# A rewritten issue order in a fused scan-attention and two-layer feed-forward kernel

## The chip, the cores and the metric

One core of one Trainium2 chip. The metric is the device time of one execution in microseconds (us), median of several runs.

## What is computed

A chunked linear attention with decay feeds two feed-forward layers. The reference, cut (4 batches, 8 heads, 768 positions, head size 32, state size 16):

```python
# attention, per chunk: Cc, Bc, xc, la = log(clip(a)), cum = cumsum(la)
M = einsum('bhin,bhjn->bhij', Cc, Bc) * exp(cum_i - cum_j) * causal
y = einsum('bhij,bhjd->bhid', M, xc) + (Cc @ state) * exp(cum)
state = exp(sum(la)) * state + sum_j Bc_j xc_j * exp(cum_last - cum_j)
# on 3072 tokens of 256 features
h = max(x @ w1, x @ w2, x @ w3)              # 768 wide
x = h @ w_out
out = (sigmoid(x @ w_gate) * (x @ w_val)) @ w_out2   # 1536 wide
```

## The kernel before, in words

The attention works on 8 chunks (c) of 96 positions. A chunk has 32 batch-heads, in 8 groups of four, so a step k = 8c + g is one group of one chunk, 64 steps in all. The feed-forward part works on 6 token tiles (t) of 512 tokens. A tile of the first layer has 6 slices (m) of 128 hidden features. Token tile 0 needs chunk 0 and the first half of chunk 1.

The attention, the preparation of the first layer's weights, token tiles 0 to 3 and the first slice of tile 4 are issued in an order written out by hand, the string `ORDER` (L52). `in_order` (L710) reads it word by word; `emit` (L655) maps a word to instructions. Each word is issued behind the last instructions of all words before it, so every engine, and SP's queue of transfers, runs its own instructions strictly in the written order, each one when its inputs and its buffer are there. The rest of token tile 4, tile 5 and the second layer follow from loops (L746, L866), which the change does not touch. The words, by engine:

- SP (SyncE), transfers: `a` loads the decays compactly, `astore` (L683) stores them clipped as the DRAM table `ad`. `LdN` (`load_decay`, L284) loads decay tile N, spread over 128 partitions; tiles 0 and 1 come from the input, the later ones from `ad`. There are four buffers of this kind, so LdN waits for the last uses of tile N-4. `LBc`, `LCc` load B and C of chunks 0 and 1, `pk` a small constant, `Lxch` (L294) x (first part) and a B layout (second part) of chunk c, half h. `Lbc` loads B and C of a later chunk, `Pdcp` (L666) distributes its bfloat16 parts. `Lwamh` (L593) loads half a weight tile of slice m in two parts.
- ACT (ScalarE): `kK` masks C for step K (L341); `Pcp` makes a bfloat16 part (L671); `sga`, `rawa`, `ra`, `hia` (L601 to L615) decode a weight tile; `H` rounds y to the high half of a split operand (L398); `E` takes a token product out of its bank (L642); `h` rounds the hidden tile (L646).
- DVE (VectorE): `clipN` clips decay tile N (L652); `DNa`, `DNb` are its two scans (L303), one for a step each; `mK` multiplies the scores of step K by the decays (L375); `T` transposes the state into the next chunk's x tile, rows of which it overwrites (L428); `X` makes the low half of y (L402); `stta` decodes weights (L609); `U`, `V` take the maximum with the other two products (L644).
- POOL (GpSimd): `bxK` state factors of step K (L364), `Q` the rest after a bfloat16 part (L673), `adda` (L612) and `loa` (L618) of weight tiles, `l` the low half of the hidden tile (L648). Those listed in `ON_DVE` run on DVE.
- PE (TensorE): `SK` the scores of step K: for k < 16 in float32 (L352), from step 16 on four bfloat16 products (L355). `yK` the outputs and state of a step (L385), from step 24 on of four steps together. `G` and `F` are the four and two terms of one token product, `N` and `O` those of the down product, all with split float32 operands (L461). `I` is an idle product on zeros and ones whose result nobody reads (L706).

Scores and token products share one pool of three PSUM banks (L348, L632), taken in turn. A bank comes free when `m`, `E`, `U` or `V` has read it. The state factors and weighed scores of a step use one of eight `mt` buffers.

Of the kernel before, what the change touches and what calls it, by code (L numbers as in the profile page):

```python
# [52 lines left out]
LB0 K Lwa00#0 a clip LC0 pk delta Lwa00 sga00 rawa00 stta00 Ld0 clip0 k6 Ld1 k2 k4 D0b S2 ra00 k5
clip1 D1a m2 adda00 I0 astore hia00 Lb2 P20 k0 D0a k1 I1 I2 Lx00#0 Lx00 bx2 Q20 k3 D1b Ld2 D2b I3
I4 I5 I6 LC1 S0 m0 S3 k7 bx3 m3 bx0 S1 m1 P21 Ld3 S5 m5 k9 I7 k8 D2a bx1 Lwa01#0 Lwa01 k13 k11 S7
loa00 D3a D3b m7 Lx01#0 sga01 rawa01 S4 m4 S6 m6 y3 Q21 Lwa10#0 Lx01 bx4 stta01 ra01 y4 Ld4 D4a y0
# [1 line left out]
Lx10#0 Lx10 y7 bx6 y6 H01 Lwa11#0 Lwa11 D5b bx11 D5a S11 S10 m11 S9 ra10 S8 T00 bx10 m10 y11 y10
adda10 Ld6 hia01 m9 bx9 y9 m8 hia10 bx8 y8 H10 Ld7 sga11 rawa11 X01 ra11 Lwa20#0 Lwa20 sga20 X10
loa10 loa01 Lwa21#0 Lwa21 D7a rawa20 D6b S13 m13 G000 F000 G001 F001 stta11 adda11 E00 sga21  # L60
rawa21 U00 ra20 Lwa30#0 Lwa30 stta20 stta21 Lx11#0 Lx11 G002 F002 G010 F010 hia11 loa11 ra21 k12
Lwa31#0 sga30 Lwa31 V00 G011 F011 G012 F012 E01 D7b bx14 h00 adda20 bx15 S12 rawa30 U01 V01 Ld8
l00 hia20 Ld9 ra30 sga31 Lx20#0 Lx20 adda21 stta30 D6a hia21 m12 Lwa41#0 loa20 rawa31 ra31 N00 O00
stta31 loa21 Lwa40#0 Lwa40 adda30 hia30 G020 F020 loa30 adda31 G021 F021 P22 k15 G022 F022 T10 h01
D8a E02 U02 bx16 V02 Lwa41 sga41 Lwa50#0 Lwa50 sga40 S14 m14 rawa40 ra40 stta40 l01 hia31 adda40
hia40 Pd21#0 S15 rawa41 loa31 G030 F030 h02 bx12 E03 Pd22#0 Pd22 N01 O01 T01 bx13 D9a bx18 G031
F031 Pd21#1 m15 y15 y13 Pd21#2 ra41 D8b bx17 sga50 l02 stta41 adda41 rawa50 ra50 stta50 loa40 U03
hia41 y12 G032 F032 N02 O02 Pd20#0 Pd20#1 Pd20#2 Pd20#3 D9b V03 Pd20#4 G040 F040 loa41 Pd20 E04
Pd21 S19 m19 S17 m17 y14 Ld10 Lwa51#0 h03 S16 G041 F041 m16 adda50 hia50 loa50 Lwa51 sga51 rawa51
D10a l03 Lx21#0 Lx21 Ld11 Lx31#0 U04 S20 m20 ra51 G042 F042 V04 h04 S18 m18 G050 F050 E05 N03 O03  # L70
S22 Lb3 stta51 S23 adda51 hia51 bx19 y18 y16 D11a Ld12 D10b bx21 m22 loa51 y17 D11b m23 y19 H11
X11 G051 F051 S21 P30 G052 F052 l04 T11 bx23 y23 Lx31 m21 bx22 H20 X20 y21 U05 bx20 y20 y22 H21
Lx30#0 X21 Q30 V05 h05 Lx30 Pd30#0 D12a bx24 Lx41#0 Lx41 N04 O04 D12b bx25 Pd30#1 Pd30#2 G100 F100
T20 G101 F101 P31 Q31 E10 U10 G102 F102 V10 P32 l05 G110 F110 E11 N05 O05 f0 Pd30#3 Ld13 Ld14 D13b
D14a D13a G111 F111 h10 G112 F112 G120 F120 l10 N10 O10 U11 V11 G121 F121 h11 l11 Pd30#4 Pd30 bx27
E12 Pd32#0 Pd31#0 Pd31#1 Pd31#2 Pd31 Pd32 S27 m27 Lb4 U12 P40 G122 F122 V12 S24 D14b Pd40#0 bx29
m24 Q40 G130 F130 N11 O11 h12 l12 G131 F131 S25 m25 E13 G132 F132 U13 V13 S26 h13 l13 P41 Pd40#1
Pd40#2 Pd40#3 m26 N12 O12 Ld15 D15a D15b bx26 G140 F140 E14 S28 m28 G141 F141 Ld16 bx31 bx28 T21
Lx40#0 Q41 Pd40#4 bx30 P42 S29 G142 F142 U14 Lx40 m29 V14 S30 m30 G150 F150 E15 Ld17 D17a S31
Pd42#0 Pd42 G151 F151 Ld18 Pd40 y27 H30 m31 bx34 y31 H31 X31 D18b X30 D16a U15 G152 F152 Pd41#0  # L80
h14 l14 N13 O13 V15 h15 Ld19 D19b D16b D19a D18a G200 F200 E20 N14 O14 G201 F201 U20 G202 F202
# [6 lines left out]
h24 Ld22 Ld23 Pd60#0 Pd60#1 l23 Pd60#2 S40 m40 G250 F250 E25 S43 G251 F251 bx41 D22a m43 T40
Pd60#3 y39 H41 X41 Pd61#0 bx43 y43 H50 X50 G252 F252 Pd61#1 N23 O23 D22b Ld24 l24 Q61 U25 V25
Pd61#2 G300 F300 S45 m45 G301 F301 N24 O24 Ld25 D24a Lx60#0 bx45 P62 h25 l25 Pd62#0 Pd62 Pd60#4  # L90
D23a E30 U30 G302 F302 V30 S44 m44 N25 O25 G310 F310 D25b D23b S47 bx46 m47 D24b h30 Pd60 G311
F311 E31 U31 S46 m46 Lb7 bx44 Pd61 l30 G312 F312 Ld26 V31 P70 f2 bx47 S51 m51 G320 F320 h31 Pd70#0
Pd70#1 Q70 Pd70#2 Pd70#3 Pd70#4 Lx60 S49 P71 G321 F321 T41 D25a Ld27 y47 E32 m49 U32 Q71 P72 bx50
G322 F322 S48 m48 Pd71#0 N30 O30 Lx61#0 V32 S50 D26b H51 m50 Lx61 G330 F330 E33 S52 D26a m52 G331
F331 X51 bx49 S53 G332 F332 bx48 m53 U33 V33 Ld28 T50 h32 D27a bx51 Ld29 S54 G340 F340 Lx70#0 m54
l31 E34 N31 O31 G341 F341 D29b bx53 Pd72#0 Pd72 S55 D27b m55 T51 h33 G342 F342 U34 V34 bx52 Pd71#1
bx54 Ld30 D30a l33 bx55 y51 y55 H61 X61 Lx70 bx59 Pd71#2 G350 F350 Pd71 l32 Pd70 S61 G351 F351
D30b m61 H60 X60 Ld31 D31b E35 U35 S63 Lx71#0 Lx71 T61 bx60 G352 F352 N32 O32 m63 G400 F400 E40
h34 D29a bx58 V35 N33 O33 D28a bx56 S56 m56 S58 l34 G401 F401 D28b m58 bx57 S57 U40 N34 O34 m57
# [874 lines left out]
```

## Time and profile before

| | before |
|---|---|
| median of 3 runs | 546.4 us (545.87 to 546.89) |
| the profiled execution | 546.38 us |
| its span, first to last instruction | 544.6 us |
| PE busy | 523.3 us (96%) |
| DVE busy | 401.1 us (74%) |
| ACT busy | 313.8 us (58%) |
| POOL busy | 90.4 us (17%) |

The profiled execution's own time is 1.8 us more than its span, which runs from its first instruction to its last. Busy time is the union of an engine's instructions. A matmul's end is modelled, so a busy PE is not PE at its peak. "Idle before" gives how long an engine stood still ahead of an instruction, and after an arrow what ended the wait.

### The profile page before, as it was taken

What the parts mean: (1) busy time and instruction counts of PE and PEld (TensorE: products, weight loads), DVE (VectorE), ACT (ScalarE), POOL (GpSimd) and SP (SyncE); (2) the same over time, 40 slices, a digit from 0 to 9 for tenths busy, and PEclk for the clock granted to TensorE, in tenths of its full rate; (3) what the DMA queues carried; (4) which work ended last, traced back from release to release, by engine and by line L of the source; (5) the groups of instructions that cost most, each with busy time, mean ns of one, the idle gap of its engine ahead of it and who ended that gap; (6) DMA issues with size and microseconds to landing.
All of it is one profiled execution on the core that took longest, in us unless ns stands there. A gap on an engine that the chain in (4) does not pass through costs nothing.

```text
span 544.6 us, 7902 instructions
## 1 busy us (share of the span) xinstructions
PE 523.3 (96%) x2897; PEld 418.2 (77%) x2898; DVE 401.1 (74%) x682; ACT 313.8 (58%) x551; POOL 90.4 (17%) x127
## 2 busy tenths in 40 slices
...
GB/s 209 289 308 214 211 158 164 162 151 138 204 182 139 222 17 201 186 46 148 78 40 0 2 0 1 1 40 39 2 0 1 0 1 78 1 0 0 2 0 78
DMA packets 33895, 50.53 MB, mean 93 GB/s; under 512 B 3392, under 2 KB 19904, under 8 KB 33856
## 3 DMA queue, kind: packets, MB, share of 16 engines
...
q8 instruction: 23, 0.38, 0.3%
...
## 4 chain that ended last, share of the span: by engine, by line
PE 82%; DVE 7%; DMA 5%; ACT 3%; issue 2%; SPq 0%; POOL 0%; DVEq 0%; POOLq 0%; ACTq 0%
PE u L461 22%; PE o L851 17%; PE ug L820 15%; PE uv L820 15%; PE o L461 7%; PE y L385 2%; PE s L352 2%; DVE dec L303 2%; PE s L355 1%; DMA bc<-in_bch 1%; DMA bx<-in_bn 1%; DMA dec<-ad 1%; DVE t_a L609 1%; DVE mt L375 1%; DVE s L644 1%
## 5 line engine op out<-in xcount | busy, mean ns | idle before, releaser
L461 PE MATMUL u<-xt_hi,w_a 128*128 128x512 f32 x432 | 121.6, 402 | 1.7 <-DVE w_a L618 0.5
L820 PE MATMUL ug<-xt_hi,w_g 128*128 128x512 f32 x252 | 92.0, 390 | 0.3 <-ACT ug L823 0.2
L461 PEld LDWEIGHTS u<-xt_hi,w_a 128*128 128x128 f32 x432 | 77.3, 188 | 19.0 <-DVE w_a L618 1.4
L820 PE MATMUL uv<-xt_hi,w_v 128*128 128x512 f32 x252 | 91.1, 390 | 0.0
L851 PE MATMUL o<-hi,w_d 128*128 128x512 f32 x288 | 78.4, 389 | 0.0
L461 PE MATMUL u<-xt_lo,w_a 128*128 128x512 f32 x216 | 66.9, 391 | 0.4 <-DVE xt_lo L402 0.4
L303 DVE TENSOR_TENSOR_SCAN dec<-dec,delta 128x388 f32<-128x388 f32 x64 | 59.5, 949 | 4.5 <-DMA dec<-ad 4.3
L851 PEld LDWEIGHTS o<-hi,w_d 128*128 128x128 f32 x288 | 54.1, 188 | 11.3
L895 DVE TENSOR_TENSOR lo<-y,hi 128x512 fp32r<-128x512 f32 x72 | 49.2, 687 | 16.1 <-ACT hi L894 15.2
L820 PEld LDWEIGHTS ug<-xt_hi,w_g 128*128 128x128 f32 x252 | 47.3, 188 | 11.2 <-ACT ug L823 0.7
L820 PEld LDWEIGHTS uv<-xt_hi,w_v 128*128 128x128 f32 x252 | 47.3, 188 | 10.7 <-DVE y L828 0.4
L894 ACT CAST hi<-y 128x512 fp32r<-128x512 f32 x72 | 44.5, 620 | 13.2 <-DVE y L891 12.0
L820 PE MATMUL ug<-xt_lo,w_g 128*128 128x512 f32 x126 | 49.1, 389 | 0.0
L820 PE MATMUL uv<-xt_lo,w_v 128*128 128x512 f32 x126 | 49.0, 389 | 0.0
L891 DVE TENSOR_TENSOR y<-uv,y 128x512 f32<-128x512 f32 x36 | 24.8, 688 | 32.9 <-PE uv L820 32.5
L461 PEld LDWEIGHTS u<-xt_lo,w_a 128*128 128x128 f32 x216 | 40.5, 188 | 9.7 <-DVE xt_lo L402 0.9
L851 PE MATMUL o<-lo,w_d 128*128 128x512 f32 x144 | 45.6, 391 | 0.0
L825 ACT COPY sv<-uv 128x512 f32<-128x512 f32 x36 | 21.2, 588 | 34.9 <-PE uv L820 34.7
L375 DVE TENSOR_TENSOR mt<-s,dec 128x384 f32<-128x384 f32 x64 | 34.6, 549 | 8.8 <-PE s L355 7.2
L644 DVE TENSOR_TENSOR s<-u,s 128x512 f32<-128x512 f32 x50 | 34.1, 682 | 8.4 <-PE u L461 7.3
L828 DVE TENSOR_TENSOR y<-ug,y 128x512 f32<-128x512 f32 x36 | 24.8, 689 | 21.0 <-ACT y L825 15.0
L461 PE MATMUL o<-hi,w_a 128*128 128x512 f32 x144 | 39.6, 397 | 0.0
...
## 6 DMA issues: line engine op xcount, KB each, us to landing
...
```

What stands on the lines that cost most here:

```text
L303: dve.tensor_tensor_scan(out=f, data0=f, data1=delta.rearrange("p u w -> p (u w)"), initial=0.0, op0=ALU.mult, op1=ALU.add)
L352: pe.matmul(ps[:, q, 0:CH], bcf[c][:, 128 * q:128 * q + 128], cm[:, k % MASKED, q], start=True, stop=True)
L375: last[0] = dve.tensor_tensor(out=m[:, :, 0:CH], in0=ps[:, :, 0:CH], in1=dc[:, :, 1:LW], op=ALU.mult)
L461: pe.matmul(ps, w[int(e == 1)], a_lo if e == 2 else a_hi, start=start, stop=stop)
L644: evict[1] = dve.tensor_tensor(out=s, in0=banks_of[t, m, 1 + (kind == "V")], in1=s, op=ALU.max)
L820: turn[0] = pe.matmul(ps, w, x, start=new and e == 0, stop=e == 2, skip_group_check=not new)
L825: evict[0] = act.copy(self.temp(1 if i == 6 else 2), ps)
L828: evict[1] = dve.tensor_tensor(out=self.t[k], in0=ps, in1=self.t[k], op=ALU.add)
L851: turn[0] = pe.matmul(acc2[t][d], w, x, start=n == 1 and e == 0, stop=n == M2 and e == 2)
L891: evict[1] = dve.tensor_tensor(out=g, in0=v, in1=g, op=ALU.mult)
L894: act.copy(hl[0], g)
L895: dve.tensor_tensor(out=hl[1], in0=g, in1=hl[0].bitcast(F32), op=ALU.subtract)
```

## The change

`ORDER` is replaced by another order of the same words; seven idle products (I6 to I12) are left out, so there are 974 words instead of 981. `ON_DVE` gets another list: 17 words instead of 15. Nothing else changes: the same transfers, scans, scores and products, with other neighbours. Where bfloat16 scores follow a token or down product, a place begins: there are 44 such places in the old order and 18 in the new one. At the start, `a`, x of chunk 0 (first half), `astore`, B, C, `pk` and decay tiles 0 and 1 now stand ahead of the first weight load. The diff, cut to the head, two stretches in the middle and at the end, and the lists:

```diff
-LB0 K Lwa00#0 a clip LC0 pk delta Lwa00 sga00 rawa00 stta00 Ld0 clip0 k6 Ld1 k2 k4 D0b S2 ra00 k5
-clip1 D1a m2 adda00 I0 astore hia00 Lb2 P20 k0 D0a k1 I1 I2 Lx00#0 Lx00 bx2 Q20 k3 D1b Ld2 D2b I3
-I4 I5 I6 LC1 S0 m0 S3 k7 bx3 m3 bx0 S1 m1 P21 Ld3 S5 m5 k9 I7 k8 D2a bx1 Lwa01#0 Lwa01 k13 k11 S7
-loa00 D3a D3b m7 Lx01#0 sga01 rawa01 S4 m4 S6 m6 y3 Q21 Lwa10#0 Lx01 bx4 stta01 ra01 y4 Ld4 D4a y0
-y2 y1 H00 X00 D4b I8 I9 Lwa10 bx7 sga10 rawa10 stta10 k14 I10 I11 LB1 I12 k10 adda01 Ld5 bx5 y5
...
-bx36 S37 m37 D17b Lx51#0 G220 F220 E22 h21 l21 S35 m35 Lx50#0 G221 F221 U22 P52 S38 m38 N20 O20
-G222 F222 S36 D20b D20a V22 h22 m36 G230 F230 E23 bx35 y35 H40 G231 F231 U23 Pd51 S39 G232 F232
...
-h35 l35 S62 D31a m62 G402 F402 S60 m60 N35 O35 bx61 T60 S59 bx63 m59 V40 bx62 y63 H71 X71 y59 H70
-X70
+a clip K Lx00#0 Lx00 astore LB0 delta LC0 pk k0 Ld0 clip0 D0a S0 m0 k6 Ld1 bx0 k2 clip1 D1a D1b
+bx3 Lwa00#0 S2 D0b k1 k4 m2 Lwa00 k3 sga00 rawa00 S1 I0 bx1 stta00 ra00 LC1 k10 adda00 k5 I1 I2 I3
+m1 k8 I4 Ld2 D2b hia00 S4 k12 D2a m4 Lb2 Ld3 D3b y1 k7 loa00 Lwa01#0 P20 Lwa01 S3 m3 S5 m5 k13 LB1
+sga01 rawa01 S7 S6 bx2 y2 Q20 P21 Q21 S8 Ld4 Ld5 Lx01#0 Lx01 k11 ra01 bx4 D3a bx6 m7 y3 y0 stta01
+m6 bx5 k9 D4b P22 Lx10#0 Lx10 S10 bx7 D4a adda01 S11 Lwa10#0 D5a m10 m8 H00 T00 X00 k15 D5b Lwa10
...
+h15 D18a Lb5 N14 D18b Pd40 P50 Q50 Lx41#0 Lx41 T31 bx36 E20 l15 G201 G202 F201 D16a bx32 O14 F202
...
+S38 m38 S36 m36 bx34 Lb6 S37 m37 Pd51#2 Pd51 Ld20 D20a D20b Pd52#0 Pd52 y35 S39 m39 h22 P60 H40
+G231 F231 G232 O21 Ld21 D21b D21a F232 U23 V23 Lx51#0 bx38 Pd60#0 Ld22 D22b Ld23 N22 Lx51 l22 Q60
...
+Pd70#0 Pd70#1 f2 G320 S50 m50 F320 E32 N30 G321 F321 Ld27 D27b Q71 bx51 bx49 Lx61#0 G322 F322 Lx61
+G330 P72 F330 E33 U32 V32 S49 m49 S54 y47 Pd71#0 Pd71#1 D27a m54 bx53 y51 Pd71#2 Pd72#0 S53 H60
+m53 H51 h31 S55 l31 D26a bx52 S52 m55 m52 O30 h32 Ld28 D28b G331 F331 N31 Ld29 D28a bx56 G332
+Lx71#0 T51 G340 F332 U33 Ld30 V33 D30b l32 O31 N32 h33 l33 F340 T60 E34 G341 F341 U34 G342 G350
+G351 Pd70#2 Pd70#3 X60 bx54 Lx71 bx55 D29a X51 Ld31 D31b F342 O32 N33 Pd70#4 V34 h34 F350 D31a
...
-ON_DVE = """Q20 loa10 adda20 adda21 loa21 adda40 l02 loa40 l05 l10 l11 l12 l21 l25 l35""".split()
+ON_DVE = """adda10 adda11 adda21 l00 loa30 adda40 l02 loa40 adda50 loa50 Q31 l12 Q41 l20 l24 l30 l33""".split()
```

## Rows read from the trace of the kernel before

**Rows 1.** The page: busy us of each engine (share of the span), instructions.
```profile
PE 523.3 (96%) x2897; PEld 418.2 (77%) x2898; DVE 401.1 (74%) x682; ACT 313.8 (58%) x551; POOL 90.4 (17%) x127
```

**Rows 2.** Table by stretch: length, busy us (instructions), clock, DMA share, GB/s.
```profile
core 0: us, PE busy (x) PEld busy (x) DVE busy (x) ACT busy (x) POOL busy (x), PEclk, DMA share, GB/s
...
11.00:79.30 68.30, 63.00 (x497) 47.94 (x498) 65.07 (x103) 45.88 (x78) 40.23 (x48) 1.00 0.82 234
79.30:209.00 129.70, 127.48 (x944) 96.85 (x942) 102.72 (x178) 44.25 (x72) 45.69 (x62) 1.00 0.70 149
209.00:545.00 336.00, 331.28 (x1456) 271.83 (x1452) 232.22 (x400) 217.55 (x390) 0.27 (x1) 1.00 0.11 38
```

**Rows 3.** Timeline of DVE: start us, duration us, instruction, [idle before <-releaser].
```profile
5.44 0.35 DVE L652 TENSOR_SCALAR a<-a 64x384 f32<-64x384 f32 x1 [5.44 <-DMA a<-in_ah]
8.46 0.69 DVE L609 SCALAR_TENSOR_TENSOR t_a<-raw_a,sg 128x512 int32<-128x512 int32 x1 [2.67 <-ACT raw_a L603]
11.08 1.19 DVE L652 TENSOR_SCALAR dec<-dec 128x768 f32<-128x768 f32 x1 [1.93 <-DMA dec<-in_ah]
```

**Rows 4.** Timeline of PE: the first products of token tiles 0 and 1.
```profile
35.12 1.18 PE L461 MATMUL u<-xt_hi,w_a 128*128 128x512 f32 x4
...
79.33 1.09 PE L461 MATMUL u<-xt_hi,w_a 128*128 128x512 f32 x4
```

**Rows 5.** Timeline of SP's queue: first issue, the decay tiles, and the store.
```profile
0.74 0.38 SPq L576 DMA_DIRECT2D y<-in_bch  x1
...
3.84 0.94 SPq L287 DMA_DIRECT2D dec<-in_ah  x2
5.82 0.48 SPq L683 DMA_DIRECT2D ad<-a  x1
```

**Rows 6.** From issue to landing: B loads (L576), compact decays (L680), decay tiles (L287).
```profile
DMA to landing us min/median/max: 2.7/3.7/4.7
...
DMA to landing us min/median/max: 3.8/3.8/3.8
...
DMA to landing us min/median/max: 3.3/5.6/7.8
```

**Rows 7.** Groups of DVE instructions: busy us, mean ns | idle before.
```profile
L303 DVE TENSOR_TENSOR_SCAN dec<-dec,delta 128x388 f32<-128x388 f32 x64 | 59.5, 949 | 4.5 <-DMA dec<-ad 4.3
...
L648 DVE TENSOR_TENSOR lo<-s,hi 128x512 fp32r<-128x512 f32 x8 | 5.4, 678 | 1.6 <-ACT hi L646 1.6
...
L612 DVE CUSTOM_DVE_ANT_0 r_a<-t_a,r_a 128x1024 uint16<-128x1024 uint16 x3 | 2.5, 830 | 0.1
...
L673 DVE TENSOR_TENSOR bc<-bc,parts 128x896 f32<-128x896 f32 x1 | 1.1, 1066 | 0.0
```

**Rows 8.** Chain of waits, token products, scores (s), outputs (y): start us, us, what.
```profile
65.96 0.28 PE s L355 x4
...
96.47 1.36 PE o L461 x6
...
99.18 0.19 PE s L355 x4
99.37 1.47 PE u L461 x6
...
198.55 0.36 PE s L355 x8
...
205.68 0.90 PE y L385 x32
206.59 1.58 PE u L461 x6
```

**Rows 9.** Waits: who waited for whom, us in total, times, the longest.
```profile
PEld L355 <- issue: 13.3, 45, 1.1
```

More of the change, by code (lines that the diff above doesn't have):

```diff
@@ L52 @@
 ORDER = """
[L53 to L56, printed above, removed]
-y2 y1 H00 X00 D4b I8 I9 Lwa10 bx7 sga10 rawa10 stta10 k14 I10 I11 LB1 I12 k10 adda01 Ld5 bx5 y5
@@ L58 @@
[L58 to L81, printed above, removed]
@@ L82 @@
-bx33 Pd41#1 Pd41#2 bx32 Pd41 S33 m33 l15 N15 O15 Lb5 P50 Q50 P51 Pd51#0 bx37 Pd50#0 V20 G210 F210
-E21 h20 l20 Q51 Pd51#1 T31 S32 m32 T30 Pd50#1 G211 F211 Ld20 S34 m34 f1 U21 G212 F212 V21 Pd51#2
-bx36 S37 m37 D17b Lx51#0 G220 F220 E22 h21 l21 S35 m35 Lx50#0 G221 F221 U22 P52 S38 m38 N20 O20
-G222 F222 S36 D20b D20a V22 h22 m36 G230 F230 E23 bx35 y35 H40 G231 F231 U23 Pd51 S39 G232 F232
-Pd52#0 Pd50#2 Ld21 Pd50#3 m39 Pd50#4 Pd50 Lx50 bx38 l22 X40 bx40 bx39 V23 N21 O21 h23 Pd52 G240
-F240 E24 S42 D21a m42 D21b N22 O22 Lb6 P60 Q60 G241 F241 U24 Lx51 S41 bx42 m41 P61 G242 F242 V24
@@ L88 @@
[L88 to L99, printed above, removed]
@@ L100 @@
-h35 l35 S62 D31a m62 G402 F402 S60 m60 N35 O35 bx61 T60 S59 bx63 m59 V40 bx62 y63 H71 X71 y59 H70
-X70
+a clip K Lx00#0 Lx00 astore LB0 delta LC0 pk k0 Ld0 clip0 D0a S0 m0 k6 Ld1 bx0 k2 clip1 D1a D1b
+bx3 Lwa00#0 S2 D0b k1 k4 m2 Lwa00 k3 sga00 rawa00 S1 I0 bx1 stta00 ra00 LC1 k10 adda00 k5 I1 I2 I3
+m1 k8 I4 Ld2 D2b hia00 S4 k12 D2a m4 Lb2 Ld3 D3b y1 k7 loa00 Lwa01#0 P20 Lwa01 S3 m3 S5 m5 k13 LB1
+sga01 rawa01 S7 S6 bx2 y2 Q20 P21 Q21 S8 Ld4 Ld5 Lx01#0 Lx01 k11 ra01 bx4 D3a bx6 m7 y3 y0 stta01
@@ new lines @@
+m6 bx5 k9 D4b P22 Lx10#0 Lx10 S10 bx7 D4a adda01 S11 Lwa10#0 D5a m10 m8 H00 T00 X00 k15 D5b Lwa10
+y4 y5 y7 y6 H01 m11 S9 sga10 S13 bx8 y8 bx10 rawa10 ra10 y10 Lwa11#0 m9 bx9 y9 Lwa11 bx11 hia01
+stta10 adda10 loa01 y11 H10 X10 I5 sga11 hia10 Ld6 D6b Lwa20#0 m13 rawa11 Lwa20 sga20 rawa20 G000
+G001 G002 Ld7 loa10 Ld8 ra11 X01 F000 F001 E00 F002 stta11 stta20 G010 F010 ra20 adda20 adda11
+hia11 loa11 hia20 loa20 U00 E01 V00 Lwa21#0 Lwa21 Lx11#0 D7b sga21 rawa21 G011 F011 U01 G012 F012
+h00 Lx11 bx13 D6a D8b Lwa30#0 ra21 Lwa30 sga30 stta21 V01 rawa30 stta30 ra30 Pd20#0 G020 F020 E02
@@ new lines @@
+adda21 Ld9 l00 bx15 G021 F021 U02 S12 m12 k14 hia21 bx12 S15 m15 Lwa31#0 Lwa31 adda30 loa21 S14
+hia30 loa30 sga31 rawa31 stta31 D7a m14 D9a G022 F022 V02 Lwa41#0 ra31 adda31 N00 h01 l01 Lwa40#0
+Lwa41 Lwa40 sga41 rawa41 O00 hia31 Lwa50#0 Lwa50 sga40 G030 G031 loa31 T01 F030 N01 O01 Pd21#0
+Pd21#1 Pd21#2 rawa40 ra40 D9b G032 stta40 adda40 y13 stta41 bx14 y14 ra41 Pd20#1 Pd20#2 y12 E03
+h02 y15 l02 F031 F032 N02 hia40 loa40 G040 F040 Pd21 sga50 rawa50 stta50 ra50 adda50 Pd22#0 O02
+U03 hia50 V03 Pd22 Pd20#3 Pd20#4 Pd20 loa50 D8a S19 m19 Lwa51#0 Lwa51 H11 X11 adda41 hia41 loa41
@@ new lines @@
+S16 m16 E04 h03 Ld10 sga51 rawa51 ra51 G041 F041 U04 stta51 l03 G042 F042 V04 h04 adda51 Lx20#0
+Lx20 hia51 S18 m18 S17 m17 N03 G050 bx19 O03 T10 bx18 F050 E05 loa51 S22 S23 bx16 Ld11 y19 D11a
+m22 y18 D11b m23 y16 S20 Lx21#0 Lx21 D10a m20 G051 bx22 F051 Lb3 P30 T11 Pd30#0 Pd30#1 Pd30#2 l04
+Q30 G052 D10b F052 bx17 N04 Ld12 S21 y22 bx23 y23 y17 bx20 y20 m21 bx21 y21 U05 H20 X20 O04 V05
+H21 X21 h05 G100 G101 F100 F101 G102 F102 N05 l05 O05 P31 Q31 P32 E10 Ld13 D13a Ld14 Ld15 D14b U10
+V10 G110 D15a Pd32#0 Pd32 F110 D14a G111 F111 E11 U11 G112 F112 G120 D12a V11 Pd31#0 Pd31#1 Pd31#2
@@ new lines @@
+G121 f0 h10 l10 h11 F120 Pd30#3 Pd31 Lx30#0 Lx30 bx24 F121 E12 U12 D13b G122 F122 l11 Pd30#4 Pd30
+Lb4 P40 Q40 P41 Lx40#0 Pd40#0 D15b N10 O10 N11 V12 D12b S24 m24 S25 S27 T20 bx27 m25 O11 m27 G130
+F130 bx25 h12 G131 G132 l12 Pd40#1 E13 Pd40#2 Ld16 Lx31#0 Pd40#3 Lx31 Pd40#4 F131 F132 N12 U13 V13
+Q41 O12 S29 m29 Pd41#0 S26 m26 D16b G140 F140 P42 S30 m30 E14 bx26 y27 S28 m28 S31 m31 bx30 G141
+bx29 G142 G150 F141 F142 F150 U14 Pd41#1 Pd41#2 V14 h14 bx28 Pd41 G151 G152 h13 Ld17 N13 bx31 D17b
+Ld18 l14 T21 H30 X30 E15 F151 F152 U15 y31 H31 Lx50#0 V15 l13 Pd42#0 Pd42 O13 Lx40 G200 X31 F200
@@ new lines @@
+h15 D18a Lb5 N14 D18b Pd40 P50 Q50 Lx41#0 Lx41 T31 bx36 E20 l15 G201 G202 F201 D16a bx32 O14 F202
+N15 U20 V20 bx33 Ld19 O15 f1 S33 m33 S34 G210 F210 T30 D17a m34 G211 F211 G212 F212 h20 l20 E21
+U21 G220 F220 bx35 V21 P51 D19b Q51 P52 S35 m35 Pd50#0 Pd50#1 E22 S32 m32 N20 G221 F221 Pd50#2
+Pd50#3 D19a Pd50#4 Pd50 G222 Pd51#0 h21 bx37 F222 U22 V22 G230 bx39 F230 E23 O20 N21 l21 Pd51#1
+S38 m38 S36 m36 bx34 Lb6 S37 m37 Pd51#2 Pd51 Ld20 D20a D20b Pd52#0 Pd52 y35 S39 m39 h22 P60 H40
+G231 F231 G232 O21 Ld21 D21b D21a F232 U23 V23 Lx51#0 bx38 Pd60#0 Ld22 D22b Ld23 N22 Lx51 l22 Q60
@@ new lines @@
+P61 Pd61#0 Q61 P62 Pd62#0 O22 Lx50 G240 F240 E24 h23 X40 Pd60#1 G241 G242 F241 U24 F242 G250 F250
+N23 D23b E25 S41 V24 S42 bx40 T40 l23 y39 bx45 bx42 H41 m42 m41 Lb7 Lx60#0 S43 m43 S40 m40 G251
+F251 Pd60#2 bx43 U25 bx41 y43 S47 m47 D22a Pd61#1 Pd61#2 S44 m44 S45 m45 O23 Lx60 H50 h24 l24 X50
+G252 F252 Ld24 N24 V25 G300 G301 Lx70#0 Lx70 X41 F300 E30 T41 F301 U30 Ld25 O24 D24a bx47 Pd60#3
+Pd60#4 bx44 G302 F302 bx48 S46 h25 l25 V30 G310 F310 G311 F311 Pd61 N25 Pd60 Pd62 D24b P70 D23a
+bx46 m46 O25 E31 U31 Ld26 D26b S51 D25b m51 Q70 P71 S48 m48 G312 F312 V31 h30 l30 T50 D25a bx50
```

7 lines of the change are left out of this document (added).

## The prediction, made before the changed kernel was run

> **What bounds the kernel now.** I read the page's busy shares first: TensorE (PE) is busy for 96% of the span, far above the other engines [rows 1]. A share of the whole span hides stages, so the table by stretch comes next. In it, from 209 us to the end, 331 of 336 us are PE work, and the change touches none of that. From 79.3 to 209 us PE is busy for 127.48 of 129.70 us and VectorE (DVE) for 102.72, so PE bounds it, with 2.2 us of idle time. From 11 to 79.3 us it is the other way round: DVE is busy for 65.07 of 68.30 us (95%) [rows 2]. So there are three questions: when does DVE get its first real work, how much does it do before the handover at 79.3 us, and how much PE time lies behind that.
>
> DVE's first work is the clip of `a` at 5.44 us and the `stt` of weight tile a00 at 8.46. Then it waits, and from 11.08 us, when decay tile 0 has landed, it hardly stops [rows 3]. The first token product (G000) starts at 35.12 us, the first of the second token tile (G100) at 79.33 [rows 4]. I take G100 as the handover.
>
> **What moves at the start.** In SP's queue the load of decay tile 0 (Ld0) is the seventh issue, at 3.84 us: six issues from 0.74 on, 0.52 us each [rows 5]. In the new order `a` is first, then the two parts of x00, then `astore`. This store waits for the clip, the clip for `a`, and SP issues in order, so LB0, LC0, pk, Ld0, Ld1 and all weights queue behind that wait. When does `a` land? Before, it took 3.8 us as third transfer; the first transfer of the queue, a larger one, took 2.7 [rows 6]. Alone on the engines, `a` is nearest to the second: 0.74 + 2.7 = 3.44, plus the clip's 0.35 gives 3.8 us. Then astore, LB0, LC0 and pk (4 x 0.52) put Ld0 at 5.9 us; with 3.8 us it is 7.0. Of landing times there are three rows: 7.2 for this tile before (11.08 - 3.84), 5.6 as the median of all decay tiles, and 3.3 to 7.8 as their ends [rows 3, 5, 6]. Ahead of it now lie x00, LB0 and LC0, about what lay ahead of it before, so I take the middle of 5.6 and 7.2. It lands at 5.9 + 6.4 = 12.3 us, **1.2 us later** than before. The ends are 5.9 + 3.3 = 9.2 (1.9 earlier) and 7.0 + 7.8 = 14.8 (3.7 later).
>
> Who waits for it: clip0, D0a, m0 and all DVE work behind them, hence every weighed score. The masks on ACT wait for LC0 and pk, which now land near 10 us instead of before 8; the scores have until 13.8 us (12.3 plus clip and scan), so that is covered. The weight loads go back by some 6 us. Weight tile a00 must be ready at G000 only, 20 us later, so DVE's scans hide it.
>
> **DVE work up to the handover.** I counted the words before G100 in both orders. The new one has 24 scans for 26 (-2 x 0.95), no subtraction of split parts on DVE for one (-1.07), five weight additions for three (+2 x 0.83) and two low halves of hidden activations for one (+0.68) [rows 7]. The stt that ran before the tile landed now runs behind it (+0.69) [rows 3]. The sum is +0.06 us, so I count nothing. G, F, N, O, S and y words before G100 are equal in number (18, 18, 5, 5, 24, 24), so the PE work behind the handover is equal too. Seven of 13 idle products go; they stand in the stretch that DVE bounds, so they save nothing. What POOL gives away (two additions) and takes (one subtraction of split parts) is hidden by its idle time, 40 of 68 us busy [rows 2].
>
> **PE work behind the handover.** The chain of waits shows the price of a place. Six token products in a row take 1.36 us. After four bf16 scores they take 1.47, and the scores 0.19; eight scores together take 0.36. So a place costs about 0.10 us on top of its scores. After a y block, six products take 1.58 us: 0.22 on top. Scores right after a y take 0.28 instead of 0.19: 0.09 on top [rows 8]. Behind G100 I count, old to new: scores followed by token products 38 to 14, y followed by token products 6 to 2, y followed by scores 0 to 6. That is 24 x 0.10 + 4 x 0.22 - 6 x 0.09 = 2.4 + 0.88 - 0.54, **2.7 us saved**. The nine old and six new breaks before G100 lie in DVE's stretch and count nothing. The bound below is nothing saved; above, 0.11 a place, 3.0 us.
>
> PE also loses its 2.2 idle us in this stretch [rows 2] to late scans, late x tiles and operand subtractions. The new order issues the part of x70 that chunk 7's state factors need far ahead of its use, but puts Lx41 right before the transposes T31 that overwrite it, behind Ld18, and Ld31 before D31b with V34 behind it on DVE. One late transfer goes, another may come: I leave the 2.2 us, with 0 and 4.5 as ends. DVE has 2.7 us more words behind G100 than before (scans that came earlier, two subtractions of split parts); with 27 idle us there [rows 2] they cost nothing unless they stand in front of a bank's release.
>
> **The sum.** +1.2 (decay tile) + 0 (DVE work) - 2.7 (places) + 0 (waits) = -1.5 us. The profiled execution took 546.38 us, 1.8 more than its span, and the median is 546.4, so the forecast is **544.9 us**. About 0.2%, 1.1 us, is what a measurement of this kernel can tell from no change: 545.3 and 547.5 us are the borders.
>
> **Rule against row.** The weight-load queue stood idle for 13.3 us in all before 45 first loads of bf16 scores, 0.3 us each, without a releaser [rows 9], and the products behind a place were late by 0.1. The Trainium skill says in "TensorE: Matmul & The Clock Gate", Step-by-step (LDWEIGHTS), that the engine pulls a weight load ahead of running matmuls. By that rule a place would cost nothing but its scores, the saving would be 0 and the time 547.6 us. By the rows it is 0.1, and I go by these.
>
> **Rivals.**
> *The queue's head takes more than the places give* (slower). SP waits for the clip with everything behind it, and the tile lands at 14.8: +3.7. T00 then also waits for Lx10, which now stands behind Ld4, Ld5 and Lx01 in SP's queue, with Ld5 held until m3; some 0.6 us more. 3.7 + 0.6 - 2.7 = +1.6, 548.0 us. It is no longer faster when the first scan's tile lands after 12.7 us (11.08 + 2.7 - 1.1), and slower after 14.9. For it: the wait was seen before (astore went out at 5.82, right behind the clip) [rows 3, 5]. Against: the transfers ahead of it are no more bytes than before. The tile alone gives "no change" with 0.2, and slower with 0.15.
> *Places are worth nothing*: the loads overlap, or bunched scores wait for banks. Scores and token products share three banks, and a run such as S49 S54 y47 y51 S53 S55 S52 needs the weighing of the score three before. Then +1.2 stays: 547.6 us. Against it: the 1.47 against 1.36 in many rows [rows 8], and y blocks or down products in most runs that give DVE time for its 0.55 us weighings. 0.08; half of the saving lost gives 546.2, "no change", 0.04.
> *The start gains too*: x00 and the scores are ready early, the tile lands by the shortest landing time (-1.9) or the 2.2 us of waits go. -1.9 - 2.7 = -4.6 or -3.7: 541.8 to 542.7 us. For it: `a`, and with it `ad`, is out sooner. 0.1.
>
> **Chances.** The forecast, 543 to 545.3 us with the tile between 10.5 and 12.7, has 0.43; with the last rival, faster has 0.53. "No change" has 0.24, slower 0.23. For 8 in 10 the range goes from 542.3, which leaves out most of the best case, to 548.0, the price of the slower rival.
>
> **What would show it.** DVE's clip of decay tile 0 near 12.3 us and SP idle before astore show the first term; G000 near 36.3 and G100 near 80.5 us show that DVE carries it on. PE from G100 to the end of the written order should take 2.7 us less than before with as much idle time, and the idle time of the weight queue before bf16 scores should fall to about 18 places. I am wrong if G100 comes before 79 us (the start is not bound by the decay tile), if idle time of PE behind it grows by over 2 us (banks, or DVE behind a transfer), or if token products behind scores still cost 0.1 us each in as many places.

## The result and the profile after

The kernel after takes 553.9 us (median of 6 runs, 550.97 to 556.85), the kernel before 545.8 us beside it. The ratio is 1.0141 with a 95% interval of 1.0106 to 1.0176, about 7.7 us **slower**. The forecast was 544.9 us, its range ended at 548.0. The profiled execution of after took 552.21 us, with a span of 550.3, the second best of the six. Lines of after are one less than those of before (L461 is L460).

The table by stretch of after, to hold against [rows 2]; the first stretch ends where the first product of token tile 1 starts:

```profile
core 0: us, PE busy (x) PEld busy (x) DVE busy (x) ACT busy (x) POOL busy (x), PEclk, DMA share, GB/s
11.00:81.40 70.40, 62.80 (x496) 49.92 (x495) 64.39 (x105) 49.36 (x84) 37.85 (x46) 0.98 0.79 238
81.40:214.70 133.30, 127.11 (x943) 98.76 (x943) 105.28 (x179) 42.39 (x70) 42.29 (x61) 1.00 0.67 146
214.70:550.00 335.30, 331.41 (x1455) 272.07 (x1453) 232.54 (x401) 218.66 (x392) 1.29 (x1) 1.00 0.11 38
```

The last stretch is as before. The handover comes 2.1 us later (81.4 for 79.33 us), and the stretch behind it is 3.6 us longer (133.30 for 129.67 from G100 to 209 us): PE does the same work there, with 6.2 us of idle time for 2.2. The clock column says 0.98 in the first stretch, where it was 1.00.

The head, to hold against [rows 3, 5]: SP's queue of after, then DVE's timeline, then PE's.

```profile
3.60 0.48 SPq L682 DMA_DIRECT2D ad<-a  x1
...
5.71 0.91 SPq L286 DMA_DIRECT2D dec<-in_ah  x2
```
```profile
3.22 0.35 DVE L651 TENSOR_SCALAR a<-a 64x384 f32<-64x384 f32 x1 [3.22 <-DMA a<-in_ah]
12.28 0.56 DVE L651 TENSOR_SCALAR dec<-dec 128x768 f32<-128x768 f32 x1 [8.71 <-DMA dec<-in_ah]
```
```profile
30.27 1.86 PE L384 MATMUL y<-mt,xs 128*32 128x112 f32 x32 [2.26 <-POOL mt L363]
...
36.45 0.73 PE L460 MATMUL u<-xt_hi,w_a 128*128 128x512 f32 x2 [0.44 <-ACT xt_hi L397]
```

The store goes out when the clip is done, LB0 and the rest behind it, Ld0 at 5.71 (forecast 5.9), and the tile's clip starts at 12.28 (forecast 12.3). G000 is 1.3 us later than before. One row was not foreseen: PE stands still for 2.26 us before 30.27. The profile puts this wait down to POOL, whose state factors of steps 4 to 7 need the transfer x01. SP issues it at 23.87 us only, behind decay tiles 4 and 5, whose issues took it from 19.32 to 23.35, and it takes 5.9 us to land. In the kernel before the same transfer went out at 15.97.

Behind the handover, who PE waits for in after, from 79 to 209 us (us in total, times, the longest), first PE, then its weight loads:

```profile
PE u L460 <- DVE s L643: 2.3, 1, 2.3
PE o L460 <- POOL lo L647: 1.8, 1, 1.8
PE s L354 <- DVE s L643: 1.0, 2, 0.6
PE y L384 <- DVE mt L374: 0.7, 1, 0.7
PE u L460 <- DVE mt L374: 0.7, 2, 0.4
```
```profile
PEld L354 <- issue: 5.7, 21, 0.7
PEld u L460 <- DVE s L643: 3.4, 3, 2.7
PEld u L460 <- DVE mt L374: 3.1, 8, 0.6
```

The weight queue's idle time before scores is 5.7 us at 21 places. In the same stretch of before it was 11.0 us at 38 places, part of the 13.3 of [rows 9]. So the places went as forecast. What grew are token products whose weight loads wait for DVE: eight times for `mt`, the weighing that frees a score's bank (3.1 us, before 0.3 and once), three times for `s` (3.4, before 0.4 and once). The two longest waits can be followed back. First the chain to 126.91 us: SP, ACT, POOL, PE, one fence each.

```profile
108.36 3.24 SPq L286 DMA_DIRECT2D dec<-ad  x2
...
114.06 0.49 SPq L584 DMA_DIRECT2D bc<-in_bch  x1
```
```profile
122.47 0.94 ACT L670 CAST parts<-bc 128x896 bf16<-128x896 f32 x1 [3.23 <-DMA bx<-in_bn]
```
```profile
123.48 1.90 POOL L672 TENSOR_TENSOR bc<-bc,parts 128x896 f32<-128x896 f32 x1 [6.54 <-ACT parts L670]
...
125.59 1.27 POOL L647 TENSOR_TENSOR lo<-s,hi 128x512 fp32r<-128x512 f32 x1
```
```profile
126.91 0.73 PE L460 MATMUL o<-lo,w_a 128*128 128x512 f32 x2 [1.81 <-POOL lo L647]
```

SP stands from 108.36 on for decay tiles 17 and 18, so the transfer of B and C for chunk 5 (Lb5, `bc`) goes out at 114.06. The trace gives it 7.9 us to landing, at 121.95. Right behind it, at 114.60, goes the last part of chunk 4 that Pd40 sends out of the buffer which ACT's P50 is to overwrite; it takes 7.7 us, to 122.3. P50 starts at 122.47, behind both, POOL's Q50 follows, and the low half l15, which needs nothing of this, stands behind Q50. The second chain ends at 195.38 us: DVE, then PE.

```profile
191.86 0.96 DVE L302 TENSOR_TENSOR_SCAN dec<-dec,delta 128x388 f32<-128x388 f32 x1 [1.99 <-DMA dec<-ad]
192.74 0.67 DVE L647 TENSOR_TENSOR lo<-s,hi 128x512 fp32r<-128x512 f32 x1
193.32 1.28 DVE L427 STREAM_TRANSPOSE xs<-y 32x128 f32<-32x128 f32 x4
194.64 0.69 DVE L643 TENSOR_TENSOR s<-u,s 128x512 f32<-128x512 f32 x1
```
```profile
195.38 1.19 PE L460 MATMUL u<-xt_hi,w_a 128*128 128x512 f32 x4 [2.28 <-DVE s L643]
```

DVE waits for decay tile 30; the scan D30b, l33 and T60 stand ahead of U34, which frees the bank that PE needs. None of them is needed so early.

### The profile page after: what moved, and what is told of

Read it like the earlier page. It is cut to its first block, busy times and chain, and to the rows that moved or that the text cites. A ratio compares the mean times of both kernels' runs of the same rounds, so it can differ in the third digit from the quotient of the medians.

```text
span 550.3 us, 7913 instructions
## 1 busy us (share of the span) xinstructions
PE 521.7 (95%) x2891; PEld 421.1 (77%) x2891; DVE 402.6 (73%) x684; ACT 313.6 (57%) x551; POOL 85.3 (15%) x125
## 4 chain that ended last, share of the span: by engine, by line
PE 69%; DMA 12%; DVE 9%; ACT 4%; SPq 3%; issue 2%; POOL 1%; DVEq 0%; POOLq 0%; ACTq 0%
PE o L850 17%; PE u L460 16%; PE ug L819 15%; PE uv L819 15%; DMA raw_a<-in_w 5%; PE o L460 5%; DVE dec L302 3%; DMA bc<-in_bch 2%; DMA dec<-ad 2%; SPq L665 2%; DVE mt L374 2%; DVE s L643 1%; DMA bx<-in_bn 1%; DVE xs L427 1%; PE y L384 1%
## 5 line engine op out<-in xcount | busy, mean ns | idle before, releaser
L460 PE MATMUL u<-xt_hi,w_a 128*128 128x512 f32 x432 | 116.7, 397 | 4.1 <-DVE s L643 2.3
L460 PEld LDWEIGHTS u<-xt_hi,w_a 128*128 128x128 f32 x432 | 79.0, 188 | 25.7 <-DVE s L643 3.4
L460 PE MATMUL u<-xt_lo,w_a 128*128 128x512 f32 x216 | 65.1, 392 | 0.0
L460 PEld LDWEIGHTS u<-xt_lo,w_a 128*128 128x128 f32 x216 | 40.3, 188 | 8.9 <-issue 0.3
L460 PE MATMUL o<-hi,w_a 128*128 128x512 f32 x144 | 39.0, 393 | 0.0
L374 DVE TENSOR_TENSOR mt<-s,dec 128x384 f32<-128x384 f32 x64 | 33.4, 550 | 6.6 <-PE s L354 4.9
```

The costliest lines, as they stand in the source:

```text
L374: last[0] = dve.tensor_tensor(out=m[:, :, 0:CH], in0=ps[:, :, 0:CH], in1=dc[:, :, 1:LW], op=ALU.mult)
L460: pe.matmul(ps, w[int(e == 1)], a_lo if e == 2 else a_hi, start=start, stop=stop)
```

## The experiments

Three theories. **W**: engines issue in order, and what PE needs stands behind a scan, a split or a store that waits for a transfer. **C**: PE pauses, its granted clock falls, and what then runs at half speed becomes the bound. **B**: scores that stand together run into the three PSUM banks, since each has to be weighed first. Ratios are against the kernel before, run beside each. The kernel after itself was timed in one set of six runs, so what an edit of it gains is the difference of two ratios, uncertain by about 2.3 us (0.0041).

### Late transfers (a_d30, a_lb5) and the seven idle products (a_idle)

Three edits of after, one each:

```diff
 a_d30
-Ld30 V33 D30b l32
+Ld30 V33 l32
...
-F341 U34 G342
+F341 U34 D30b G342
 a_lb5
-h13 Ld17 N13
+h13 Lb5 Ld17 N13
...
-D18a Lb5 N14
+D18a N14
 a_idle
-adda01 S11 Lwa10#0
+adda01 S11 I6 I7 I8 I9 I10 I11 I12 Lwa10#0
```

> Theory W (engines that run in order stand behind late transfers): moving the scan D30b behind U34 takes away the 2.3 us for which PE waited at 192.7 us; profiled time some 2 us below that of the changed kernel (552.2 us, median 553.9), with no idle PE over 1 us between 185 and 200 us. Theory C (the lowered clock at the start costs the time): no change, within the changed kernel's own spread of 551 to 557 us. Theory B (bunched scores starve the three banks): the wait comes back at the same product, no change.

> Theory W: with the load Lb5 in front of Ld17 and Ld18 in SP's queue, its data are there some 5 us earlier, P50 and Q50 no longer hold up ACT and POOL, and the 1.8 us for which PE waited at 124.7 us for the low half l15 go; about 2 us less than the changed kernel. Theory C: no change. Theory B: no change, the wait at 134 us for banks stays as it is.

> Theory C: with the seven idle products put back, in the pause of PE behind S11 (28 to 30 us), the granted clock stays at 1.00 (2.4 GHz) from its first rise, the spread of the runs shrinks from 6 us to about 1 us, and the median falls by 2 to 3 us (553.9 to about 551.5). Theory W: waits from 79 us on are as before, 550.5 to 552 us at best, since the profiled run with hardly a lowered clock took 552.2. If the idle products do nothing, the median stays near 553.9 with the same spread.

a_d30: 551.0 us, 1.0091 (1.0069 to 1.0113). PE's wait of 2.28 us for U34 is gone; on its weight queue 0.45 us of 2.70 are left. The other waits stayed. a_lb5: 551.9 us, 1.0107 (1.0084 to 1.013). PE's wait for l15 fell from 1.81 to 0.24 us, but another came ahead of it. Decay tile 17 now lands behind Lb5; DVE waits for it with the scan D17b, the transposes T21 stand behind the scan, and y31 on PE behind them. DVE, then PE:

```profile
115.02 0.96 DVE L302 TENSOR_TENSOR_SCAN dec<-dec,delta 128x388 f32<-128x388 f32 x1 [2.56 <-DMA dec<-ad]
```
```profile
117.26 0.97 PE L384 MATMUL y<-mt,xs 128*32 128x112 f32 x32 [1.44 <-issue]
```

B and C of chunk 5 land 8 us earlier than in after, at 114.0, yet P50 starts at 121.23, 1.24 us earlier, behind Pd40's last part (issued at 113.03, 7.9 us to landing). So Lb5 was not alone in holding P50, and in this profile the wait moved more than it went. The wait for U34 stayed, with something behind it that the profile of after does not have. PE's timeline of a_lb5, then the table by stretch, where the clock is the column behind PE's busy time (it is 1.00 in the stretches around this one):

```profile
194.66 1.20 PE L460 MATMUL u<-xt_hi,w_a 128*128 128x512 f32 x4 [2.02 <-DVE s L643]
...
197.17 1.91 PE L460 MATMUL o<-hi,w_a 128*128 128x512 f32 x4
```
```profile
196.00:199.30 3.30, 3.30 (x9) 0.50 0.00 0
```

After the pause of 2.02 us the clock is at half, 1.2 GHz, for 3.3 us, and four products take 1.91 us where they take about 1.1 elsewhere. So a pause can cost more than its length. a_idle: 551.2 us (549.11 to 552.24), 1.0089 (1.0065 to 1.0112): seven products on constants, which do nothing, take back about half a per cent. In its profiled run the clock fell all the same, behind y1's pause of 2.24 us and for 6.7 us. So a_d30 speaks for W (0.0050 of the ratio) and a_idle for C (0.0052), each just clear of the 0.0041; the 0.0034 of a_lb5 is not.

### The three together (a_all)

With l20 off the list `ON_DVE`, so that POOL does it; why l20, the last section shows.

```diff
-Q41 l20 l24
+Q41 l24
```

> All three edits, and l20 moved from VectorE to POOL (it took 1.9 us beside POOL's Q51 where such an instruction takes 0.7). Theory W with C: the four effects add up, -2.3 -1.8 -1.2 for the waits at 192.7, 124.7 and 133 to 135 us, -2 for the clock: about 546.5 us, with a spread of 1 us. Theory C alone: 551.5 us. Theory B: banks take over, not below 550 us.

548.9 us (548.02 to 550.9), 1.0048 (1.0029 to 1.0067). The waits at 126.9, 134 and 195 us are gone, others of 0.2 to 1.1 us stand in new places (one is y31's behind D17 again, 1.09 us). Two thirds of the loss are taken back, less than the three edits add up to one by one (0.0136 of the ratio for 0.0093).

### The wait for the clip (a_head), and its surprise

a_all, with the store behind Ld1:

```diff
-Lx00 astore LB0
+Lx00 LB0
...
-Ld1 bx0
+Ld1 astore bx0
```

> a_all (the new order with D30b behind U34, Lb5 ahead of Ld17, I6 to I12 kept and l20 on POOL: 548.9 us) with one more move: astore stands behind Ld1, so that LB0, LC0, pk and Ld0 no longer stand behind a wait for the clip in SP's queue. Theory W (in-order engines stand behind late transfers): Ld0 is issued at 4.0 to 4.5 us instead of 5.7, decay tile 0 lands at 10.8 to 11.2 instead of 12.3, G000 and G100 come 1.0 to 1.3 us earlier, 547.6 us. Rival (the start is held by something other than the tile's issue, a later transfer or PE's clock): the clip of decay tile 0 comes earlier but G100 does not, 548.5 to 549 us.

547.7 us (546.55 to 551.55), 1.0034 (1.0013 to 1.0056). DVE of a_head, then PE's timeline, then its stretches:

```profile
9.67 0.56 DVE L651 TENSOR_SCALAR dec<-dec 128x768 f32<-128x768 f32 x1 [6.14 <-DMA dec<-in_ah]
...
28.43 1.02 DVE L374 TENSOR_TENSOR mt<-s,dec 128x384 f32<-128x384 f32 x2 [2.21 <-PE s L351]
...
34.70 0.56 DVE L374 TENSOR_TENSOR mt<-s,dec 128x384 f32<-128x384 f32 x1 [1.94 <-PE s L351]
```
```profile
16.75 0.40 PE L384 MATMUL y<-mt,xs 128*32 128x112 f32 x8 [2.13 <-issue]
```
```profile
14.70:16.70 2.00, 0.00 (x0) 1.00 0.86 322
18.60:32.10 13.50, 13.50 (x75) 0.50 0.88 269
...
52.70:56.00 3.30, 3.30 (x12) 0.50 0.98 133
```

The tile comes 1.4 us earlier than even in the kernel before, and in this run nothing of it reaches the handover (82.0 us, 81.9 in a_all): PE pauses for 2.1 us ahead of y1, its clock falls for 13.5 us in which it is busy throughout, and DVE, the bound of this stretch in [rows 2], waits twice for scores, 4.2 us in all. This profiled run shows the rival's case, the clock. The median is the one that W forecast, but its ratio is not told apart from a_all's (1.0034 and 1.0048).

### The kernel before without idle products (b_noidle), with scores in pairs (b_pair), with two waits taken out (b_fix)

Edits of before: I0 to I12 dropped; eight bfloat16 scores moved up, each directly behind another; two words moved.

```diff
 b_noidle
-m2 adda00 I0 astore
+m2 adda00 astore
...
 b_pair
-S28 m28 G141
+S28 S29 m28 G141
...
-P42 S29 G142
+P42 G142
...
 b_fix
-D18b X30 D16a
+X30 D18b D16a
...
-m32 T30 Pd50#1
+m32 Pd50#1
...
-V21 Pd51#2
+V21 T30 Pd51#2
```

> The kernel before, without its 13 idle products; nothing else moves. Theory C (a clock that falls in the first 35 us because PE pauses there is part of the loss): the granted clock falls to half for some us before 30 us, and the time rises by 0.5 to 2 us, 546.5 to 548. Theory W: VectorE bounds the first 79 us, so even a halved clock there costs less than 0.5 us, 545.8 to 546.4.

> The kernel before, with eight bfloat16 scores moved up to stand directly behind another score, so that eight places between token products go and nothing else moves. By the price of a place (0.10 us, nothing given back) 0.8 us less, 545.1 us. Theory B (scores that stand together run into the three PSUM banks, because VectorE has to weigh each before its bank is free): the product behind each pair waits 0.3 to 0.5 us for its bank, more than the place was worth, 547.5 to 549 us, with PE idle 2 to 4 us more between 79 and 209 us.

> The kernel before, with two words moved by theory W: the subtraction X30 ahead of the scan D18b, and the transposes T30 behind V21, so that two of its own waits of PE for VectorE in the bounded stretch (0.6 us at 116 and 1.6 us near 127.5) should go. Theory W: PE idle between 79.3 and 209 us falls from 2.2 us to about 0.5, 544.4 us. Rival: the waits reappear at the next place that needs VectorE, 545.5 to 546 us.

b_noidle: 551.2 us (551.03 to 551.32), **1.0094** (1.0067 to 1.0121). Its stretches:

```profile
20.40:27.10 6.70, 4.52 (x69) 1.00 0.96 328
27.20:34.00 6.80, 5.98 (x46) 0.50 0.62 181
```

The clock falls as C says, and the loss is over twice what even C expected; the handover is 2.2 us late, and another 2 us came near 93 us, where PE waits for a transfer of B and C (1.0 us), as it does in b_fix (1.15), which has its idle products; so that part need not come from their loss. Idle products are no free padding, though DVE has the largest busy share there.

b_pair: 547.7 us (546.78 to 549.57), 1.0027 (1.001 to 1.0045), slower where eight places fewer should have saved 0.8 us. PE's timeline has what theory B says:

```profile
104.06 1.19 PE L461 MATMUL u<-xt_hi,w_a 128*128 128x512 f32 x4 [0.32 <-ACT s L642]
...
180.09 1.19 PE L461 MATMUL u<-xt_hi,w_a 128*128 128x512 f32 x4 [0.48 <-DVE mt L375]
```

A place costs 0.1 us, the wait behind a pair 0.3 to 0.5. b_fix: 547.3 us (546.32 to 548.64), 1.0017 (0.9999 to 1.0036), a miss: the wait at 116 us went, those near 129 stayed in part (0.89 for 1.03 us), and waits of 0.65 for a low half and 0.72 for a weighing came up beside them. The rival's mechanism held, though the time is above its range too; the 1.15 us for a transfer, at 94 us, came ahead of both edits and is not theirs.

### Holding the clock (c_clk, c_aclk, c_best, b_q)

c_aclk is after with one edit, the idle product I5 and seven more ahead of y1, the first pause. c_clk is a_head with that edit, its idle products behind S11 taken for it. c_best is c_clk with l00 on POOL and O04 ahead of y21. b_q is before with decay tile 0 ahead of the first weight tile, and that tile's decode behind the first scan.

```diff
 c_aclk
-D3b y1
+D3b I5 I6 I7 I8 I9 I10 I11 I12 y1
 c_clk
-D3b y1
+D3b I5 I6 I7 I8 I9 I10 I11 I12 y1
...
-S11 I6 I7 I8 I9 I10 I11 I12 Lwa10#0
+S11 Lwa10#0
 c_best
-m21 bx21 y21 U05 H20 X20 O04 V05
+m21 bx21 O04 y21 U05 H20 X20 V05
 b_q
-LB0 K Lwa00#0 a clip LC0 pk delta Lwa00 sga00 rawa00 stta00 Ld0 clip0 k6 Ld1 k2 k4 D0b S2 ra00 k5
+LB0 K a clip LC0 pk Ld0 Lwa00#0 delta Lwa00 clip0 k6 Ld1 k2 k4 D0b S2 sga00 rawa00 stta00 ra00 k5
```

> a_head with its idle products I5 to I12 in front of y1, where PE pauses for 2.1 us (14.6 to 16.8 us in a_head) just before the granted clock falls to half for 13.7 us, in place of behind S11 and X10. Nothing else moves. Theory C (the clock that falls behind this pause makes PE the bound of the start): the clock stays full from 12 to 50 us, VectorE's two waits of 2.2 and 1.9 us for scores go, G100 comes 1.5 to 2.5 us earlier, 545.5 us. Theory W alone: the clock may stay up, but G100 stays where it is, 547.7 us.

> The kernel after with this one edit alone (eight idle products in front of y1; all late transfers and the wait for the clip stay). Theory C: the runs lose their low-clock stretches before 35 us; that is worth 1 to 2 us, 552.3 us, and the spread of the runs (551 to 557) shrinks. Theory W alone: 553.9 us, the same spread.

> c_clk with two more words moved: the low half l00 goes from VectorE to POOL (on VectorE it took 1.76 us beside a POOL instruction, 0.68 elsewhere, with the scores of chunk 1 waiting 1.6 us for its bank behind it), and the down products O04 stand in front of y21, where PE waits 0.7 us for VectorE. Theory W: both waits go, PE no longer pauses at 50 us, 0.7 to 1.3 us less than c_clk, 544.5 us, a version that beats both kernels. Rival (other waits take their place): as c_clk.

> The kernel before, with decay tile 0 issued in front of both halves of the first weight tile (fifth in SP's queue, near 2.9 us, and its weight's stt behind the first scan). If the landing of decay tile 0 sets the end through VectorE, as the prediction had it: it lands 1 to 2.4 us earlier (8.7 to 10 us), VectorE takes over the 0.7 us of the stt, the end comes 0.5 to 1.7 us earlier, 545.2 us. Rival (the start is held elsewhere, by scores, masks or weights, as a_head suggests, where the tile came 1.4 us earlier than in the kernel before and G100 did not): 546 to 547 us.

c_aclk: 551.9 us (549.19 to 553.15), 1.0089 (1.0062 to 1.0116). c_clk: 547.9 us (545.31 to 550.24), 1.0014 (0.9999 to 1.0029), a miss. The profiles show why; this is the stretch in question in c_aclk:

```profile
30.80:40.90 10.10, 9.50 (x65) 0.50 1.03 342
```

Behind the first pause, of which 1.26 us are left, the clock stays up, but behind S11 stands a second one, for POOL's state factors of steps 4 to 7, which wait for x01 (the 2.26 us of after; 1.55 here), and the clock falls there, in c_clk too. In the profiled run of after it had also fallen at the second pause only, for 3.3 us, so these two profiles alone do not show what the edit gains. c_best: 547.6 us (545.09 to 549.31), 1.0009 (0.9992 to 1.0026). Its profiled run had the full clock throughout and took 545.1 us; the median was no better than c_clk's.

b_q: 548.7 us (546.49 to 549.74), 1.0039 (1.0025 to 1.0053), another miss. DVE's and PE's timelines:

```profile
7.73 0.56 DVE L652 TENSOR_SCALAR dec<-dec 128x768 f32<-128x768 f32 x1 [2.87 <-DMA dec<-in_ah]
...
10.93 0.69 DVE L609 SCALAR_TENSOR_TENSOR t_a<-raw_a,sg 128x512 int32<-128x512 int32 x1 [1.56 <-ACT raw_a L603]
```
```profile
15.26 0.96 PE L352 MATMUL s<-y 128*128 128x96 f32 x3 [3.86 <-ACT y L341]
```

Decay tile 0 is there 3.35 us earlier than in [rows 3], and DVE then stands behind the first weights, and for scores that wait for masks. Here a tile that comes earlier gains nothing and lengthens PE's pause; as the first weights moved back for it, this is not a test of the tile alone.

### Both pauses filled, and the clip's price (d_aclk, d_fin, d_clip)

d_aclk is c_aclk, d_fin is c_best, each with seven more idle products behind S11. d_clip is d_fin with the store back where the change has it.

```diff
 d_aclk
-adda01 S11 Lwa10#0
+adda01 S11 I13 I14 I15 I16 I17 I18 I19 Lwa10#0
 d_clip
-Lx00 LB0
+Lx00 astore LB0
...
-Ld1 astore bx0
+Ld1 bx0
```

> The kernel after with idle products at both of its early pauses of PE, eight in front of y1 and seven more behind S11 (where PE waits 1.6 to 2.3 us for POOL's states of chunk 4, which wait for x01's transfer); c_aclk filled the first alone, and its clock fell at the second. All late transfers and the wait for the clip stay. Theory C: the clock stays full from 14 us to at least 50 us, and G100 comes 2 to 4 us earlier than in c_aclk; the waits behind 125 us stay; 549.5 us. Theory W: as c_aclk, 551.9 us, or as the kernel after, 553.9 us.

> c_best with seven more idle products behind S11, the place where its remaining pause of 1.3 us stood and where c_clk's clock fell. Theory C: all runs are then like the best of c_best (545.1 to 545.3 us at clock 1.0), so the median falls from 547.6 to 545.2 us, the spread halves, and it beats the kernel before. Rival (the spread of c_best has another cause, such as the times at which transfers land): median 547 to 548 us, with low-clock stretches absent and late transfers in the trace.

> d_fin with astore back in front of LB0, as the change has it, so that everything behind it in SP's queue waits for the clip again. With the clock held, this prices the first term of the forecast alone. Theory (the start then is bound by VectorE from decay tile 0 on): the tile lands 1.2 to 2 us later than in d_fin and the end follows, 546.2 to 547.2 us. Rival (the start is held by scores and their clock): as d_fin, within 0.5 us.

d_aclk: 550.6 us (549.98 to 553.31), 1.007 (1.0048 to 1.0092). The clock stays up:

```profile
16.00:79.00 63.00, 57.14 (x462) 1.00 0.81 223
```

PE's waits behind the handover are those of after (1.49 for l15, 1.94 for U34). Idle products alone thus give back half of the loss in the medians (1.0141 to 1.007). In the profiled runs it is less, 1.4 us; after's was one of its better ones: its mean clock was 0.996, and the run with the lowest one, 0.981, took 556.9 us.

d_fin: 546.8 us (545.3 to 547.43), 0.9999 (0.9985 to 1.0014). The spread halves against c_best (2.1 for 4.2 us) and the long runs are gone, but the median is that of the kernel before, not 545.2. No version beat both kernels. d_clip: 547.9 us (546.69 to 550.38), above the range expected, 1.0026 (1.0011 to 1.0041). The clip of decay tile 0 in d_fin and in d_clip:

```profile
10.53 0.56 DVE L651 TENSOR_SCALAR dec<-dec 128x768 f32<-128x768 f32 x1 [6.59 <-DMA dec<-in_ah]
```
```profile
12.19 0.56 DVE L651 TENSOR_SCALAR dec<-dec 128x768 f32<-128x768 f32 x1 [8.65 <-DMA dec<-in_ah]
```

1.66 us between the tiles, 1.5 us between the ratios (0.0027), uncertain by 1.1: with the clock held, this fits what the prediction took the start for, DVE from decay tile 0 on. The two profiled runs differ by more than the tile (G100 at 78.84 and 81.42 us, spans of 543.6 and 548.1); d_clip's is one of its longest, and the rest of the difference is not traced.

## Why the prediction was wrong

Taken back one after another, with differences of the ratios: idle products in both pauses 3.9 us (1.0141 to 1.007, d_aclk), late transfers, low halves and O04 2.4 us (to 1.0026, d_clip), the store behind the clip 1.5 us (to 0.9999, d_fin). They are uncertain by about 2.3, 1.5 and 1.1 us, and another order of the edits would share the sum out otherwise (a_d30 alone gave 2.7 us). Together they are all of the 7.7 us. It also means that the 2.7 us of the places never arrive.

**The decay tile, +1.2 us: right.** 12.28 for 12.3, and 1.5 us, uncertain by 1.1, by d_clip. What was argued for it (astore behind the clip, the queue behind astore) is in SP's rows. G100 came 2.1 us late in the profiled run, 0.9 more than that, and DVE had waited 1.22 us for decay tile 5 at 28.8 us.

**The places, -2.7 us: right as a price, wrong in the sum.** The weight queue's idle time before scores halved with the number of places, and a place that is left costs what it did. In d_fin, four products behind scores, then four behind products:

```profile
128.59 1.17 PE L460 MATMUL o<-hi,w_a 128*128 128x512 f32 x4
...
130.98 1.07 PE L460 MATMUL u<-xt_hi,w_a 128*128 128x512 f32 x4
```

But scores that stand together put waits for banks behind them (theory B; b_pair shows it alone). In d_fin, from G100 to the end of the written order, PE needs 129.0 us where it needed 129.7, with 2.0 and 2.2 us idle. The rest of the saving went into token products that start late: their weight loads wait 2.3 us for `s` and 2.1 us for `mt`, at ten places, where before it was 0.7 us at two. The rival that named this, places worth nothing, had 0.08. It had two conditions, loads that overlap and bunched scores that wait for banks; the second took the saving. The rule on weight loads that the prediction quotes from the Trainium skill ("TensorE: Matmul & The Clock Gate", Step-by-step (LDWEIGHTS)) gave the same 547.6 us, but did not take it: the 0.1 us stayed.

**Idle products, 0 us: failed.** The step read "they stand in the stretch that DVE bounds, so they save nothing", and did not ask what they cost when they go. They cover PE's pauses at the start, and the new order has pauses of its own there: y1 waits for DVE's weighing m1, the states of steps 4 to 7 wait for x01. About half of the loss hangs on the clock (a_idle, c_aclk, d_aclk from after; b_noidle from before), 3.9 us with 2.3 either way. A stretch that DVE bounds at 2.4 GHz can be bound by PE at 1.2 (a_head, 18.6 to 32.1 us).

**Waits behind the handover, 0 us: failed.** "One late transfer goes, another may come: I leave the 2.2 us, with 0 and 4.5 as ends." They are 6.2 us in the profiled run. The two late transfers that the text looked at (Lx41, Ld31) were none of them; those that counted were Ld30, just ahead of the scan that waits for it, and Lb5 with Pd40 behind it. Of the two, a_d30 shows the first; how much of the second is Lb5's, a_lb5 leaves open. The upper end took one new wait to be worth as much as the old ones; there were two of about 2 us, two of some 0.5 us behind l20, and the bank waits. The test that would have shown the error stood in the text: "idle time of PE behind it grows by over 2 us (banks, or DVE behind a transfer)". It did, for both reasons.

**The low half on DVE, +0.68: failed in size.** l00 took 1.76 us, and l20, which the sum left out as work behind the handover, 1.92; each stands ahead of a bank's release.

The clock and the waits behind transfers were no rival's case. The slower rival, the queue's head alone, got its mechanism and 1.5 of the 7.7 us.

Open: how d_fin's 546.8 us divides between late transfers and bank waits, and why runs of c_best with a full clock differ by 3 us. Not tried: x01 ahead of decay tiles 4 and 5 in SP's queue, which would take the second pause away instead of filling it, and P50 and Q50 behind l15.
